# A width-3 convolution by minimal filtering: F(6,3) over 342 tiles in place of F(4,3) over 512

## The chip, the cores and the metric

The kernel runs on one core of a Trainium2 chip. The metric is the device time of one execution in microseconds (us); it was timed in three runs. One further execution was taken by the hardware profiler, and everything below that speaks of a start, a duration or a wait comes from that execution. The engines are named as the profile names them: PE (TensorE, matrix products), PEld (its weight loads), DVE (VectorE), ACT (ScalarE), POOL (GpSimd) and SP (SyncE, which here only issues DMAs).

## The reference

`x` is two sequences of 2048 positions with 1024 channels, bf16; `w` has three taps of 1024x1024. A convolution along the sequence is followed by a batch normalisation and SiLU:

```
xp = pad(x, one position before and after)
y  = sum over k = 0, 1, 2 of  xp[:, k:k+2048, :] @ w[k]
y  = (y - mean) * (g / sqrt(var + 1e-5)) + b
return silu(y)
```

## The kernel before

**The method.** Four neighbouring outputs of a width-3 filter need 12 products of a position with a tap. F(4,3) gets them from 6: each tile of 6 neighbouring positions is combined into 6 sums with the numbers of `BT`, the three taps are combined into 6 weight sums, the 6 pairs are multiplied, and the 4 outputs are sums of the 6 products. Each "product" here is a matrix product over 1024 input channels, done as 8 matrix instructions (one per 128 channels, variable `ct`). A sequence of 2048 has 512 tiles, the two together 1024 (`NT`).

**The first stage** (lines 178 to 233) makes the sums of x. 34 windows of 126 positions are loaded, one DMA each. `Rm` holds the numbers of `BT` laid out for 31 tiles, and a product of the window with `Rm` (line 205, 8 per window) both transposes the window and makes its 6 sums. DVE and ACT share out the copies of the results from PSUM (the banks PE writes) to `T_sb` in SBUF as bf16, two copies of 744 columns per window (lines 217 and 219).

**The weights.** Output channels are worked in 8 chunks of 128 (`dc`). For each chunk the three taps are loaded (`load_weights`, line 133) and POOL makes four weight sums from them (`transform_weights`, line 146): six additions or subtractions of 1024 columns and two multiplications by 2 and 4. The first and last weight sum are the plain taps. The sums live in a pool of two buffers, so those of chunk d+1 can be made while PE works on chunk d.

**The second stage** (lines 288 to 350) goes through units: one unit is one chunk and one block of 512 tiles, so there are two units to a chunk. The very last block is cut into two of 256 tiles. In a unit PE forms the six products `M[1], M[2], M[3], M[4], M[0], M[5]`, 8 instructions of 512 columns each (line 316), in six PSUM banks. ACT copies `M[1]` and `M[3]` to SBUF, DVE combines them with the other products in ten instructions (lines 320 to 337), writing two of the sums back over `M[2]` and `M[4]` in PSUM, and ACT applies scale, bias and SiLU into `yT` (line 306, four instructions). Every one of the ten DVE instructions has one input in PSUM and one in SBUF, or both in PSUM.

**The way out.** `yT` has channels on partitions, the output has positions there. A transposing DMA turns each unit into `o_sb` (line 251), and four DMAs store it (line 247), row by row of the four outputs of a tile. The last two units are transposed by PE instead (line 265) and copied out by DVE and ACT. SP issues these DMAs and the later weight loads in an order that the code fixes with `sp_chain`. A scheduler places the rest: it may move an instruction ahead of others in an engine's queue, and each engine then works its queue strictly in order.

Of the kernel before, what the change touches and what calls it, by code (L numbers as in the profile page):

```python
# [9 lines left out]
ALU = mybir.AluOpType  # L10
# [3 lines left out]

BT = [
    [4, 0, -5, 0, 1, 0],
    [0, -4, -4, 1, 1, 0],
    [0, 4, -4, -1, 1, 0],
    [0, -2, -1, 2, 1, 0],
    [0, 2, -1, -2, 1, 0],  # L20
    [0, 4, 0, -5, 0, 1],
]
KAPPA = [1.0 / 24.0, 1.0 / 12.0, 1.0 / 6.0, 1.0 / 6.0]
WT = 31
# [3 lines left out]
def kernel(  # L28
# [16 lines left out]
    assert S % 4 == 0 and C % P == 0 and D % P == 0  # L45
    NTB = S // 4
    NT = B * NTB
    NWIN = (NTB + WT - 1) // WT
    NBLK = min(512, NT)
    assert NT % NBLK == 0 and NBLK % P == 0  # L50
    NNB = NT // NBLK

# [12 lines left out]
    val = consts.tile([P, 6, WT], I32, name="val")  # L65
    nc.gpsimd.iota(val, pattern=[[-1, 6], [-4, WT]], base=0, channel_multiplier=1)
    E = consts.tile([P, 6, WT], FP32, name="E")
    nc.vector.tensor_single_scalar(E, val, 0.0, op=ALU.is_equal)
    Rm = consts.tile([P, 6, WT], BF16, name="Rm")
    nc.vector.memset(Rm, 0.0)  # L70
    for k in range(6):
        j = 0
        while j < 6:
            v = BT[j][k]
            if v == 0:
                j += 1
                continue
            j1 = j
            while j1 + 1 < 6 and BT[j1 + 1][k] == v:
                j1 += 1  # L80
            nj = j1 - j + 1
            nc.vector.scalar_tensor_tensor(
                out=Rm[:, j:j1 + 1, :],
                in0=E[:, k:k + 1, :].to_broadcast([P, nj, WT]) if nj > 1 else E[:, k:k + 1, :],
                scalar=float(v),
                in1=Rm[:, j:j1 + 1, :],
                op0=ALU.mult,
                op1=ALU.add,
            )
            j = j1 + 1  # L90

# [3 lines left out]
    def load_params(dep=None):  # L95
        prm = consts.tile([P, 4, DC], BF16, name="prm")
        for q, ap in enumerate((var, g, mean, b)):
            d = nc.sync.dma_start(out=prm[:, q, :], in_=ap.rearrange("(dc p) -> p dc", p=P), allow_slow_non_contiguous=True)
            after(d, dep, "param loads happen after the x window loads")
# [3 lines left out]
        nc.gpsimd.tensor_scalar(rstd, prm[:, 0, :], 1e-5, 1.0, op0=ALU.add, op1=ALU.mult)  # L103
        nc.gpsimd.tensor_tensor(rstd, rstd, mhalf, op=ALU.pow)
        sc = consts.tile([P, DC], FP32, name="sc")
        nc.gpsimd.tensor_tensor(sc, prm[:, 1, :], rstd, op=ALU.mult)
        beta = consts.tile([P, DC], FP32, name="beta")
        nc.gpsimd.tensor_tensor(beta, prm[:, 2, :], sc, op=ALU.mult)
        nc.gpsimd.tensor_tensor(beta, prm[:, 3, :], beta, op=ALU.subtract)
        sk = consts.tile([P, DC, 4], FP32, name="sk")  # L110
        for i in range(4):
            nc.gpsimd.tensor_scalar(sk[:, :, i], sc, KAPPA[i], 0.0, op0=ALU.mult, op1=ALU.add)
        return sk, beta

    w_all = w.rearrange("k (ct p) d -> p k ct d", p=P)
    raw = {}
    SYNC_DEP = mybir.DependencyInfo(mybir.DependencyClass.Sync, mybir.DependencyReason.DATA)

    def after(inst, dep, why):
        if dep is not None:  # L120
            tc.add_manual_dep(inst.ins, dep.ins.name, SYNC_DEP, reason=why)


    NOSYNC_DEP = mybir.DependencyInfo(mybir.DependencyClass.NoSync, mybir.DependencyReason.DATA)
    sp_last = [None]

    def sp_chain(inst):
        if sp_last[0] is not None:
            tc.add_manual_dep(inst.ins, sp_last[0].ins.name, NOSYNC_DEP, reason="keep SP DMA issue order")
        sp_last[0] = inst  # L130
        return inst

    def load_weights(dc, dep=None, eng=None, chain=False):
        wch = wpool.tile([P, 3, CT, P], BF16, name="wch")
        if eng is None:
            d = nc.gpsimd.dma_start(out=wch, in_=w_all[:, :, :, dc * P:(dc + 1) * P])  # L136
            after(d, dep, "weight chunk load must not compete with the x window loads")
        else:
            for k in range(3):
                d = eng.dma_start(out=wch[:, k], in_=w_all[:, k, :, dc * P:(dc + 1) * P])  # L140
                after(d, dep, "weight chunk load must not compete with the x window loads")
                if chain:
                    sp_chain(d)
        raw[dc] = wch

    def transform_weights(dc):
        wch = raw[dc]
        uch = upool.tile([P, 4, CT, P], BF16, name="uch")
        g32 = wtmp.tile([P, CT, P], FP32, name="g32")
        f32 = wtmp.tile([P, CT, P], FP32, name="f32")  # L150
        w1x2 = wtmp.tile([P, CT, P], BF16, name="w1x2")
        w2x4 = wtmp.tile([P, CT, P], BF16, name="w2x4")
        w0, w1, w2 = wch[:, 0], wch[:, 1], wch[:, 2]
        nc.gpsimd.tensor_tensor(g32, w0, w2, op=ALU.add)  # L154
        nc.gpsimd.tensor_tensor(uch[:, 0], g32, w1, op=ALU.add)
        nc.gpsimd.tensor_tensor(uch[:, 1], g32, w1, op=ALU.subtract)
        nc.gpsimd.tensor_scalar(w2x4, w2, 4.0, 0.0, op0=ALU.mult, op1=ALU.add)
        nc.gpsimd.tensor_scalar(w1x2, w1, 2.0, 0.0, op0=ALU.mult, op1=ALU.add)  # L158
        nc.gpsimd.tensor_tensor(f32, w0, w2x4, op=ALU.add)
        nc.gpsimd.tensor_tensor(uch[:, 2], f32, w1x2, op=ALU.add)  # L160
        nc.gpsimd.tensor_tensor(uch[:, 3], f32, w1x2, op=ALU.subtract)
        wts[dc] = (wch, uch)

    wts = {}

    T_sb = tpool.tile([P, CT, 6, NT], BF16, name="T_sb")
    CH = 4
    NGRP = 4
    grp_i = 0
    eng_load = {"act": 0.0, "dve": 0.0}  # L170
    EVAC_COST = {"act": 0.80, "dve": 0.95}
    sk = beta = None
    win_i = 0
    xw0 = consts.tile([P, C], BF16, name="xw0")
    nc.gpsimd.memset(xw0[0:1, :], 0.0)
    evacs = []
    NW_TOTAL = B * NWIN
    W0_AFTER = min(8, NW_TOTAL - 1)
    with tc.tile_pool(name="xwin", bufs=12) as xpool:
        for bi in range(B):  # L180
            for wi in range(NWIN):
                ntile = min(WT, NTB - WT * wi)
                n0 = bi * NTB + WT * wi
                t_lo = 4 * WT * wi - 1
                t_hi = 4 * WT * wi + 4 * ntile
                lo = max(t_lo, 0)
                hi = min(t_hi, S - 1)
                p_lo = lo - t_lo
                kk = hi - t_lo + 1
                hi_ld = min(t_lo + P - 1, S - 1)  # L190
                if p_lo > 0:
                    hi_ld = min(hi_ld, lo + 125)
                if p_lo > 0:
                    assert p_lo == 1
                    xw = xw0
                else:
                    xw = xpool.tile([P, C], BF16, name="xw")
                nc.sync.dma_start(out=xw[p_lo:p_lo + (hi_ld - lo + 1), :], in_=x[bi, lo:hi_ld + 1, :])
                win_i += 1
                for h in range(CT // CH):  # L200
                    gi = grp_i % NGRP
                    grp = ps_all[:, gi * 1024:(gi + 1) * 1024].rearrange("p (s e) -> p s e", e=256)
# [181 lines left out]
```

## Time and profile before

| | us |
|---|---|
| three runs, median (lowest to highest) | 211.66 (210.42 to 212.34) |
| span of the profiled execution, first to last instruction | 207.6 |
| median of the runs less that span | 4.06 |
| first product of the second stage starts | 34.86 |
| PE busy | 194.5 (94% of the span) |
| DVE busy | 130.2 (63%) |
| POOL busy | 124.4 (60%) |
| ACT busy | 95.7 (46%) |

The page gives the profiled execution's span and no separate time for it, so what lies around the span is read from the difference to the median of the runs. Rows of a timeline give the start and the duration in us, then engine, line, operation, the tile written and the tiles read, and the count of equal instructions merged into the row. An instruction's duration contains a fixed part that overlaps the next instruction, so two instructions of 0.69 can start 0.60 apart. What a stream of instructions costs is the distance of the starts.

### The profile page before, as it was taken

How to read it: one execution, taken by the hardware profiler on the slowest of the kernel's cores; microseconds unless marked ns; L12 is line 12 of the kernel's file. 1: busy time of each engine (PE TensorE's matmuls, PEld its weight loads, DVE VectorE, ACT ScalarE, POOL GpSimd, SP SyncE). 2: the span in 40 equal slices, each digit the busy share in tenths (PEclk: the TensorE clock that was granted, in tenths of full speed). 3: DMA queues.
4: the chain of work that ended last, by engine and by line, in shares of the span. 5: the costliest groups of instructions: out<-in, count | busy, mean ns of one | idle time of the engine just before them, and what ended most of it. 6: DMA issues, size and time to landing. Idle time of an engine off the chain costs nothing.

```text
span 207.6 us, 3056 instructions
## 1 busy us (share of the span) xinstructions
PE 194.5 (94%) x1104; PEld 104.4 (50%) x1104; DVE 130.2 (63%) x225; ACT 95.7 (46%) x142; POOL 124.4 (60%) x83
## 2 busy tenths in 40 slices
PE   2998788999999999999999999999999999999980
PEld 2977676444444444444444444444444444446870
DVE  5899697292929292929292929292929292929671
ACT  4799697234343434343434333333434343434651
POOL 4030299999999999969925992499469910000000
PEclk9999999999999999999999999999999999999998
DMA  6999972995456945794569457945794545454562
GB/s 190 380 334 312 327 282 2 157 148 104 101 103 156 197 104 101 167 188 101 104 154 200 101 101 167 190 103 101 176 178 104 101 101 101 101 104 101 103 147 56
DMA packets 96035, 31.40 MB, mean 151 GB/s; under 512 B 91606, under 2 KB 91606, under 8 KB 96020
## 3 DMA queue, kind: packets, MB, share of 16 engines
q1 hardware_dynamic: 95812, 30.42, 65.6%
q0 software_dynamic: 208, 0.79, 1.4%
q8 instruction: 8, 0.13, 0.3%
q14 instruction: 7, 0.06, 0.1%
HBM read 14.95 MB, written 8.39 MB: 112 GB/s over the span
## 4 chain that ended last, share of the span: by engine, by line
PE 85%; DMA 6%; ACT 5%; DVE 1%; issue 0%; ACTq 0%; DVEq 0%
PE ps_all L316 79%; ACT T_sb L217 5%; PE ps_all L205 5%; DMA xw<-in_x_dram 5%; DMA xw_105<-in_x_dram 1%; PE ps_all L265 0%; ACT yT L306 0%; ACTq L379 0%; DVE y_1946 L337 0%; DVE cp L325 0%; DVE ps_all L326 0%; DVE y_1946 L331 0%; DVE y_1944 L329 0%; DVE y_1945 L327 0%; DVE o_sb L273 0%
## 5 line engine op out<-in xcount | busy, mean ns | idle before, releaser
L316 PE MATMUL ps_all<-T_sb,uch 128*128 128x512 bf16 (+1 forms) x544 | 113.7, 366 | 0.1
L316 PEld LDWEIGHTS <-uch 128*128 128x128 bf16 x544 | 53.1, 98 | 57.6 <-issue 0.3
L316 PE MATMUL ps_all<-T_sb,wch 128*128 128x512 bf16 (+1 forms) x272 | 58.1, 366 | 0.0
L316 PEld LDWEIGHTS <-wch 128*128 128x128 bf16 x272 | 26.6, 98 | 28.7
L219 DVE CAST T_sb<-ps_all 128x744 bf16<-128x744 f32 (+1 forms) x31 | 26.7, 906 | 4.9 <-PE ps_all L205 4.4
L217 ACT CAST T_sb<-ps_all 128x744 bf16<-128x744 f32 (+1 forms) x37 | 26.7, 786 | 6.3 <-PE ps_all L205 5.8
L205 PE MATMUL ps_all<-Rm,xw 126*128 126x186 bf16 (+1 forms) x256 | 25.4, 250 | 3.8 <-ACT T_sb L217 1.9
L205 PEld LDWEIGHTS <-xw 126*128 126x128 bf16 (+1 forms) x256 | 22.2, 101 | 7.0 <-issue 4.1
L154 POOL TENSOR_TENSOR g_208<-wch 128x1024 f32<-128x1024 bf16 x1 | 2.1, 2115 | 10.0 <-DMA wch<-in_w_dram 10.0
L136 POOL DMA_DIRECT2D wch<-in_w_dram x1 | 1.6, 1639 | 10.3 <-ACT T_sb L217 10.3
L205 PE MATMUL ps_all<-Rm,xw_105 126*128 126x186 bf16 x16 | 2.5, 299 | 3.8 <-DMA xw_105<-in_x_dram 3.7
L158 POOL TENSOR_SCALAR w1x_1291<-wch 128x1024 bf16<-128x1024 bf16 x1 | 1.0, 1045 | 6.0 <-DMA wch<-in_w_dram 6.0
L158 POOL TENSOR_SCALAR w1x_1466<-wch 128x1024 bf16<-128x1024 bf16 x1 | 1.0, 1044 | 5.7 <-DMA wch<-in_w_dram 5.7
L158 POOL TENSOR_SCALAR w1x_1637<-wch 128x1024 bf16<-128x1024 bf16 x1 | 1.0, 1045 | 4.5 <-DMA wch<-in_w_dram 4.5
L205 PEld LDWEIGHTS <-xw_105 126*128 126x128 bf16 x16 | 1.7, 118 | 3.9 <-POOL mhalf L101 3.7
L265 PE MATMUL ps_all<-ident,yT 128*128 128x128 bf16 x16 | 1.6, 220 | 1.6 <-ACT yT L306 1.6
L320 DVE TENSOR_TENSOR bp<-S_582,ps_all 128x512 f32<-128x512 f32 x1 | 0.7, 689 | 3.4 <-PE ps_all L316 3.4
L154 POOL TENSOR_TENSOR g_1464<-wch 128x1024 f32<-128x1024 bf16 x1 | 2.1, 2122 | 1.0 <-DMA wch<-in_w_dram 1.0
L154 POOL TENSOR_TENSOR g_1114<-wch 128x1024 f32<-128x1024 bf16 x1 | 2.1, 2125 | 0.3 <-issue 0.3
L306 ACT ACTIVATE yT<-y_588,beta,sk 128x512 bf16<-128x512 f32 x1 | 0.8, 812 | 3.2 <-DVE y_588 L327 3.2
L158 POOL TENSOR_SCALAR w1x_1116<-wch 128x1024 bf16<-128x1024 bf16 x1 | 1.0, 1046 | 2.0 <-DMA wch<-in_w_dram 2.0
L306 ACT ACTIVATE yT<-y_662,beta,sk 128x512 bf16<-128x512 f32 x1 | 0.8, 815 | 3.1 <-DVE y_662 L327 3.1
(351 smaller groups left out, 301.7 us busy)
## 6 DMA issues: line engine op xcount, KB each, us to landing
xw<-in_x_dram SPq DMA_DIRECT2D x30, 256.0 KB, 6.0
out_dram<-o_sb SPq DMA_DIRECT2D x60, 128.0 KB, 2.2
wch<-in_w_dram SPq DMA_DIRECT2D x21, 256.0 KB, 4.3
wch<-in_w_dram POOLq DMA_DIRECT2D x1, 768.0 KB, 11.5
out_dram<-o_sb SPq DMA_DIRECT2D x8, 64.0 KB, 1.7
xw_105<-in_x_dram SPq DMA_DIRECT2D x2, 252.0 KB
xw<-in_x_dram SPq DMA_DIRECT2D x2, 130.0 KB
o_sb<-yT SPq DMA_TRANSPOSE x15, 4.3
```

The costliest lines, as they stand in the source:

```text
L136: d = nc.gpsimd.dma_start(out=wch, in_=w_all[:, :, :, dc * P:(dc + 1) * P])
L154: nc.gpsimd.tensor_tensor(g32, w0, w2, op=ALU.add)
L158: nc.gpsimd.tensor_scalar(w1x2, w1, 2.0, 0.0, op0=ALU.mult, op1=ALU.add)
L205: nc.tensor.matmul(grp[:, c4, 0:6 * ntile], lhsT=xw[0:kk, ct * P:(ct + 1) * P], rhs=Rm[0:kk, :, 0:ntile], start=True, stop=True,)
L217: ev = nc.scalar.copy(dst, src)
L219: ev = nc.vector.tensor_copy(dst, src)
L265: nc.tensor.transpose(bank_v[:, a, ns, :], yT[:, i, ns * P:(ns + 1) * P], ident)
L306: nc.scalar.activation(yT[:, i, :], src, ACT.Silu, bias=beta[:, dc:dc + 1], scale=sk[:, dc, i:i + 1])
L316: nc.tensor.matmul(M[j], lhsT=lhsT, rhs=T_sb[:, ct, j, nsl], start=(ct == 0), stop=(ct == CT - 1))
L320: nc.vector.tensor_tensor(bp, S1, M[2], op=ALU.subtract)
```

## The change

F(6,3) takes tiles of 8 positions and gets 6 outputs from 8 products. A sequence has 342 tiles (2052 positions, four of them past the end), and a unit is now one chunk and one sequence. The parts:

- `BT` is an 8x8 table, windows hold 21 tiles (still 34 windows), `T_sb` is one tile per sequence with 8 sums.
- Six weight sums are made instead of four. POOL's part is eight additions or subtractions of 1024 columns; the three multiplications go to ACT (`nc.scalar.mul`), the sum `e1` of the outer taps to DVE. For the first chunk DVE does the multiplications and POOL `e1`.
- A unit has 64 matrix instructions of 342 columns in eight PSUM banks, which is all of them. ACT copies three products at once (`Acp`, 1026 columns). DVE forms `S_ = Acp + M` and `D_ = Acp - M` for three pairs at once, in SBUF; twelve `scalar_tensor_tensor` instructions (`stt`, line 268) then make the six outputs from slices of `S_` and `D_`, each reading two SBUF tiles; two additions bring in the products of banks 6 and 7.
- Two SiLU instructions of 3x342 columns write `yT` with the six outputs of a tile interleaved, so that `yT` is in the order of the sequence. The transposing DMA then gives blocks of 128 positions. The SiLU of `D_`'s outputs and the way out are put behind the next unit's `Acp` copy (`late`). The last unit is not cut in two; PE transposes it.
- The first chunk's weights are loaded by SP behind the third window (before: by POOL after eight windows), the parameters by row and transposed by PE, the first window in two DMAs; the manual ordering of DMAs is gone.

The core of the diff:

```diff
 def transform_weights(dc, first=False):
-        nc.gpsimd.tensor_tensor(g32, w0, w2, op=ALU.add)
-        nc.gpsimd.tensor_tensor(uch[:, 0], g32, w1, op=ALU.add)
-        nc.gpsimd.tensor_tensor(uch[:, 1], g32, w1, op=ALU.subtract)
-        nc.gpsimd.tensor_scalar(w2x4, w2, 4.0, 0.0, op0=ALU.mult, op1=ALU.add)
-        nc.gpsimd.tensor_scalar(w1x2, w1, 2.0, 0.0, op0=ALU.mult, op1=ALU.add)
-        nc.gpsimd.tensor_tensor(f32, w0, w2x4, op=ALU.add)
-        nc.gpsimd.tensor_tensor(uch[:, 2], f32, w1x2, op=ALU.add)
-        nc.gpsimd.tensor_tensor(uch[:, 3], f32, w1x2, op=ALU.subtract)
+        for dst, src, f in ((w2x4, w2, 4.0), (w0x4, w0, 4.0), (w1x2, w1, 2.0)):
+            if first:
+                nc.vector.tensor_scalar(dst, src, f, 0.0, op0=ALU.mult, op1=ALU.add)
+            else:
+                nc.scalar.mul(dst, src, f)
+        (nc.gpsimd if first else nc.vector).tensor_tensor(e1, w0, w2, op=ALU.add)
+        nc.gpsimd.tensor_tensor(e2, w0, w2x4, op=ALU.add)
+        nc.gpsimd.tensor_tensor(eh, w0x4, w2, op=ALU.add)
+        for s, op in ((0, ALU.add), (3, ALU.subtract)):
+            nc.gpsimd.tensor_tensor(uch[:, s + 0], e1, w1, op=op)
+            nc.gpsimd.tensor_tensor(uch[:, s + 1], e2, w1x2, op=op)
+            nc.gpsimd.tensor_tensor(uch[:, s + 2], eh, w1x2, op=op)
...
+    def stt(o, i0, s, i1):
+        nc.vector.scalar_tensor_tensor(out=o, in0=i0, scalar=s, in1=i1, op0=ALU.mult, op1=ALU.add)
+
+    units = [(dc, bi) for dc in range(DC) for bi in range(B)]
+    late = []
+    for ui, (dc, bi) in enumerate(units):
...
+        for k, j in enumerate(JA):
+            mms(k, j, dc, bi)
+        nc.scalar.copy(Acp, banks(0, 3))
+        for f in late:
+            f()
+        late = []
+        for k, j in enumerate(JB):
+            mms(3 + k, j, dc, bi)
+        nc.vector.tensor_tensor(S_, Acp, banks(3, 3), op=ALU.add)
+        nc.vector.tensor_tensor(D_, Acp, banks(3, 3), op=ALU.subtract)
+        mms(6, 0, dc, bi)
+        mms(7, 7, dc, bi)
+        for par, src, y in ((0, S_, yS), (1, D_, yD)):
+            for q in range(3):
+                i = 2 * q + par
+                stt(y[:, q], src[:, 1], ALPHA * 2.0 ** i, src[:, 0])
+                stt(y[:, q], src[:, 2], BETA * 0.5 ** i, y[:, q])
+            if par == 0:
+                nc.vector.tensor_tensor(y[:, 0], bank[6], y[:, 0], op=ALU.add)
+                silu(0, yS)
+            else:
+                nc.vector.tensor_tensor(y[:, 2], bank[7], y[:, 2], op=ALU.add)
```

How it moves the queues, at three places. First DVE, from the last copies of the first stage to the end of the first unit, before:

```order
L219 CAST T_sb<-ps_all 128x24x31 x14
L219 CAST T_sb<-ps_all 128x24x16
L320 TENSOR_TENSOR bp<-S_582,ps_all 128x512
L321 TENSOR_TENSOR ps_all<-S_582,ps_all 128x512
L325 TENSOR_TENSOR cp<-S_583,ps_all 128x512
L326 TENSOR_TENSOR ps_all<-S_583,ps_all 128x512
L327 TENSOR_TENSOR y_588<-cp,ps_all 128x512
```

and the same place after the change, where `e_706` and `e_919` are the sums `e1` of the second and the third chunk of weights (one buffer for all of them):

```order
L228 CAST T_sb_138<-ps_all 128x32x6
L141 TENSOR_TENSOR e_706<-wch 128x1024
L141 TENSOR_TENSOR e_919<-wch 128x1024
L296 TENSOR_TENSOR S__617<-Acp,ps_all 128x1026
L297 TENSOR_TENSOR D__618<-Acp,ps_all 128x1026
L268 SCALAR_TENSOR_TENSOR yS<-S__617 128x342 x2
L268 SCALAR_TENSOR_TENSOR yS<-S__617,yS 128x342 x2
L268 SCALAR_TENSOR_TENSOR yS<-S__617 128x342
L306 TENSOR_TENSOR yS<-ps_all,yS 128x342
L268 SCALAR_TENSOR_TENSOR yS<-S__617,yS 128x342
```

The weight sums of two later chunks have come to stand ahead of the first unit's work, and the one input in PSUM that every DVE instruction had is gone from the twelve `L268`. Second, POOL over one chunk of weights in the second stage, before:

```order
L154 TENSOR_TENSOR g_764<-wch 128x1024
L157 TENSOR_SCALAR w2x_767<-wch 128x1024
L158 TENSOR_SCALAR w1x_766<-wch 128x1024
L159 TENSOR_TENSOR f_765<-wch,w2x_767 128x1024
L155 TENSOR_TENSOR uch<-g_764,wch 128x1024
L156 TENSOR_TENSOR uch<-g_764,wch 128x1024
L160 TENSOR_TENSOR uch<-f_765,w1x_766 128x1024
L161 TENSOR_TENSOR uch<-f_765,w1x_766 128x1024
```

and after, for the second and the beginning of the third chunk:

```order
L142 TENSOR_TENSOR e_707<-wch,w2x_711 128x1024
L143 TENSOR_TENSOR eh<-w0x_710,wch 128x1024
L145 TENSOR_TENSOR uch<-e_706,wch 128x1024
L146 TENSOR_TENSOR uch<-e_707,w1x_709 128x1024
L147 TENSOR_TENSOR uch<-eh,w1x_709 128x1024
L145 TENSOR_TENSOR uch<-e_706,wch 128x1024
L146 TENSOR_TENSOR uch<-e_707,w1x_709 128x1024
L147 TENSOR_TENSOR uch<-eh,w1x_709 128x1024
L142 TENSOR_TENSOR e_920<-wch,w2x_924 128x1024
```

The two short multiplications have left POOL and two additions have come; `e_706` is read last by the sixth of the eight, so `e_919`, which takes its buffer, waits for that one. Third, DVE at the start, where the table `Rm` is built, after the change:

```order
L92 SCALAR_TENSOR_TENSOR Rm<-E,Rm 128x21 x6
L138 TENSOR_SCALAR w2x_258<-wch 128x1024
L92 SCALAR_TENSOR_TENSOR Rm<-E,Rm 128x126
L138 TENSOR_SCALAR w0x_257<-wch 128x1024
L138 TENSOR_SCALAR w1x_256<-wch 128x1024
```

A multiplication that waits for the first weights now stands ahead of the last instruction that fills `Rm`, without which PE cannot begin the first stage.

More of the change, by code (lines that the diff above doesn't have):

```diff
@@ L78 @@
             j1 = j
-            while j1 + 1 < 6 and BT[j1 + 1][k] == v:
+            while j1 + 1 < 7 and BT[j1 + 1][k] == v:
                 j1 += 1
@@ L109, in load_params @@
[L109 to L121, printed above, removed]
@@ L124 @@
[L124 to L144, printed above, removed]
@@ L351, with banks, store @@
-    for st, _ in pending:
-        emit_output_stage_pe(st, 0, last=True)
-        emit_output_stage_pe(st, 1, last=True)
+    out_f = out.flatten_outer_dims()
+    bank = [ps_all[:, i * 512:i * 512 + NTB] for i in range(8)]
+    def banks(i0, n):
+        return ps_all[:, i0 * 512:(i0 + n) * 512].rearrange("p (k e) -> p k e", e=512)[:, :, 0:NTB]
+    def store(st, k0, nk):
+        o_sb, dc, bi = st
+        r0 = bi * S + k0 * P
+        dst = out_f[r0:r0 + nk * P, dc * P:(dc + 1) * P].rearrange("(k p) d -> p k d", p=P)
+        nc.sync.dma_start(out=dst, in_=o_sb[:, k0:k0 + nk])
```

344 lines of the change are left out of this document (155 added, 189 removed), and 8 rows, old and new, of the table BT.

## The prediction

> **What bounds the kernel now.** I read the page's busy rows and its chain of work first, then the chain in order of time, then the timeline of one unit, and last the few instructions that resemble those the change brings.
>
> ```profile
> PE 194.5 (94%) x1104; PEld 104.4 (50%) x1104; DVE 130.2 (63%) x225; ACT 95.7 (46%) x142; POOL 124.4 (60%) x83
> PE 85%; DMA 6%; ACT 5%; DVE 1%; issue 0%; ACTq 0%; DVEq 0%
> ```
>
> ```profile
> 0.73 2.88 DMA xw_105<-in_x_dram
> 3.61 0.14 issue
> 3.75 4.51 PE ps_all L205 x28
> ...
> 14.63 10.10 DMA xw<-in_x_dram
> ...
> 34.86 161.67 PE ps_all L316 x776
> 196.54 0.22 PE ps_all L265 x4
> 196.76 1.75 PE ps_all L316 x16
> ```
>
> From 34.86 on the chain is one unbroken run of products: PE bounds the second stage, and nothing stands between its products. The first 34.9 us are loading x and copying its sums. How much a column costs PE is read from two equal points of neighbouring units, the ACT copies of `M[1]`:
>
> ```profile
> 47.78 0.56 ACT L318 COPY S_656<-ps_all 128x512 f32<-128x512 f32 x1
> ...
> 58.14 0.56 ACT L318 COPY S_735<-ps_all 128x512 f32<-128x512 f32 x1
> ```
>
> 10.36 us for 48 instructions of 512 columns is 215.8 ns each; the 16 of 256 columns above took 1.75, 109.4 ns each. Between them lie 0.416 ns a column, so 342 columns should take 109.4 + 86 x 0.416 = 145.1 ns.
>
> **PE's part.** 1024 instructions (8 chunks, 2 sequences, 64) by 145.1 ns are **148.6 us**, 9.29 a unit and 18.6 a chunk. Before, from 34.86 to the end of the last product, it was 166.5:
>
> ```profile
> 199.44 1.91 PE L316 MATMUL ps_all<-T_sb,wch 128*128 128x256 bf16 x16
> ```
>
> This ends at 201.35. If PE stays the bound the products save 17.9 us. Whether it stays the bound is decided by DVE and POOL.
>
> **DVE and POOL per chunk.** One stretch with both at work:
>
> ```profile
> 49.16 0.69 DVE L320 TENSOR_TENSOR bp<-S_656,ps_all 128x512 f32<-128x512 f32 x1 [2.25 <-PE ps_all L316]
> 49.72 2.13 POOL L156 TENSOR_TENSOR uch<-g_561,wch 128x1024 bf16<-128x1024 f32 x1
> 49.76 0.69 DVE L321 TENSOR_TENSOR ps_all<-S_656,ps_all 128x512 f32<-128x512 f32 x1
> 51.81 2.12 POOL L159 TENSOR_TENSOR f_562<-wch,w2x_564 128x1024 f32<-128x1024 bf16 x1
> ...
> 187.68 0.69 DVE L326 TENSOR_TENSOR ps_all<-S_1782,ps_all 128x512 f32<-128x512 f32 x1
> ```
>
> ```profile
> 200.05 0.42 DVE L326 TENSOR_TENSOR ps_all<-S_1940,ps_all 128x256 f32<-128x256 f32 x1
> 200.38 0.41 DVE L327 TENSOR_TENSOR y_1945<-cp,ps_all 128x256 f32<-128x256 f32 x1
> ```
>
> DVE starts are 0.60 apart for 512 columns and 0.33 for 256, so 0.42 for 342, and 1.14 for 1024 or 1026. A unit has two of 1026 and fourteen of 342: 2 x 1.14 + 14 x 0.42 = 8.2; a chunk has two units and one `e1`, 17.5. POOL starts are 2.09 apart; eight are 16.7 a chunk. Against PE's 18.6 each of the two fits, with 1.1 and 1.9 to spare: taken one by one, PE stays the bound. ACT, with two `Acp`, four SiLU and three multiplications of about 1.2 each (0.82 for 512 columns, below), has some 11 a chunk and doesn't matter.
>
> But the two do not work on separate data paths for certain. Before, every DVE instruction of the second stage has an input in PSUM; the 0.69 beside POOL's 2.13 is the 0.69 of 187.68, where POOL has long been done, so such pairs don't disturb DVE. The twelve `L268` a unit and `e1` read two SBUF tiles while POOL reads two as well. The trace has one kind of DVE instruction with two SBUF inputs, the sixteen that build `Rm`, and just one POOL instruction that reads SBUF beside them:
>
> ```profile
> 1.92 0.18 DVE L82 SCALAR_TENSOR_TENSOR Rm<-E,Rm 128x31 bf16<-128x31 f32 x1
> ```
>
> ```profile
> 2.27 0.44 POOL masks.py:199 TENSOR_SCALAR_AFFINE_SELECT ident<-ident 128x128 bf16<-128x128 bf16 x1
> 2.35 0.21 DVE L82 SCALAR_TENSOR_TENSOR Rm<-E,Rm 128x62 bf16<-128x62 f32 x1
> ...
> 2.49 0.27 DVE L82 SCALAR_TENSOR_TENSOR Rm<-E,Rm 128x31 bf16<-128x31 f32 x1
> ```
>
> The instruction of 31 columns takes 0.18 next to a POOL memset (which writes only) and 0.27 inside POOL's select (the 0.21 there has twice the columns). One event of 0.09 us, short, but in the only place where it could show. So I bound the pairing from both sides: at the least nothing, at the most full exclusion, in which DVE's two-SBUF instructions and POOL's never run together. Per chunk that is 16.7 for POOL and 24 x 0.42 + 1.14 = 11.2 for DVE, **27.9 in sequence instead of 18.6**. DVE's other instructions (4 x 1.14 + 4 x 0.42 = 6.2) can hide beside POOL. A gain is excluded. I take the upper end, since the one row that bears on it shows a wait, and a wait that lasts as long as POOL is reading lasts nearly all of the 2.13 us here, whereas the select reads 128 columns once.
>
> [...]
>
> It applies to the weight sums of chunks 3 to 8, made while DVE works on the units of chunks 1 to 7; those of the last chunk leave the final chunk's units free, and those of the second are made largely while DVE waits (next part). That leaves six chunks at 27.9: 6 x 9.3 = **+55.8**.
>
> **The queue of DVE at the turn of the stages.** `e_919` stands ahead of the first `S_` and needs the buffer that POOL's sixth instruction of the second chunk reads last. POOL's chain there begins after ACT's first multiplication behind the last copy (about 1.2), so with products from 35: 35 + 1.2 + 6 x 2.09 = 48.7, then `e_919` 1.14 and `S_`, `D_` 2.28, which is 52.1. PE needs the banks that these free when it comes to the second three products of the second unit, at 35 + 9.3 + 3.5 = 47.8. It waits 4.3, and once more 1.2 at bank 7, which DVE frees 5.9 after 52.1, where PE arrives 4.7 after it. Together **+5.5**. Queued behind `e_919` is all of DVE's work. Bounds: nothing, if POOL starts earlier, and 8.
>
> **The first stage.** The x windows bring the same bytes, and the chain waits on them for 10.10. The copies have 672 columns instead of 744:
>
> ```profile
> L217 ACT CAST T_sb<-ps_all 128x744 bf16<-128x744 f32 x35 | 25.8, 803 | 6.2 <-PE ps_all L205 5.8
> L219 DVE CAST T_sb<-ps_all 128x744 bf16<-128x744 f32 x29 | 25.8, 930 | 4.9 <-PE ps_all L205 4.4
> ```
>
> A tenth off each is 2.6 us. Against it, `Rm` is finished only after the first weights have landed:
>
> ```profile
> wch<-in_w_dram SPq DMA_DIRECT2D x21, 256.0 KB, 4.3
> ```
>
> They are issued when the first window has landed (3.6), so PE begins at about 7.9 instead of 3.75, 4.2 later, while the twelve window buffers go on filling. I put the first product at **35.0**; bounds 33 (the load is hidden) and 39 (all 4.2 added).
>
> **The end.** The last unit is no longer halved. DVE starts on it when sixteen products (2.3 us) are still to come and needs 8.2, so 5.9 after PE's end; then:
>
> ```profile
> 191.66 0.82 ACT L306 ACTIVATE yT<-y_1788,beta,sk 128x512 bf16<-128x512 f32 x1
> 192.38 0.80 ACT L306 ACTIVATE yT<-y_1785,beta,sk 128x512 bf16<-128x512 f32 x1
> ...
> 197.72 0.58 ACT L270 COPY o_sb<-ps_all 128x512 bf16<-128x512 bf16 x1
> ...
> 203.31 0.40 PE L265 MATMUL ps_all<-ident,yT 128*128 128x128 bf16 x4 [0.93 <-ACT yT L306]
> 203.74 0.49 DVE L273 COPY o_sb<-ps_all 128x256 bf16<-128x256 bf16 x2 [0.90 <-PE ps_all L265]
> ```
>
> Two SiLU of 513 columns 1.5, eight transposes 0.8, one copy 0.6, and from the last copy (204.2) to the end of the span 3.4: **12.2**, where 6.3 stood (201.35 to 207.6).
>
> **The sum.** 35.0 + 148.6 + 55.8 + 5.5 + 12.2 = 257.1 as a span, against 207.6. The median of the runs lies 4.06 above the span: 261.2, rounded **261**. Parameters, the interleaved `yT` and the DMAs cost nothing here: a transposing DMA and four stores per unit as before, one unit's time (9.3 or more) to hide in.
>
> **The rivals.**
>
> *DVE and POOL do not disturb each other.* For it: one event of 0.09 us is thin, and the instruction of 0.21 ran inside the same select unharmed. Then 35.0 + 148.6 + 5.5 + 12.2 = 201.3, with 4.1 a time of **205**, 3% faster. It decides at 18.6 a chunk: if a chunk stays below 19.7, the change wins.
>
> *They share, but finer than by whole instructions.* For it: the wait was shorter than the select. Half of the 55.8 gives **233**, slower.
>
> *No disturbance, but DVE becomes the bound by itself.* An instruction that needs the result of the one before it can't use the overlap: 0.42 against a distance of 0.33, 0.09 lost. With ten such in a unit, 8.2 + 0.57 + 0.9 = 9.7 exceeds PE's 9.29 by 0.4, over 16 units 6: **211**, no change. Against it: the scheduler has put other instructions between most of these pairs.
>
> **How the numbers follow.** A measurement of this kernel can tell about 1% from no change. Full exclusion 0.52, sharing 0.14, no disturbance 0.28, DVE alone 0.06: slower 0.66, same 0.06, faster 0.28. The likeliest case's own range is 246 (an exclusion with a quarter of it lost between) to 274 (two us more a chunk, where POOL waits for PE's release of a buffer while DVE has nothing to do). The range has to take in the faster case too: 203 to 274.
>
> **What would show it.** Right: `L268` has a median well above 0.42, some of its instructions over 2 us; POOL's eight are stretched or DVE waits beside them; PE's idle time in the second stage is tens of us, ended by DVE (`S_`, or a bank it frees); six chunks take about 28 and the last one less than 20. `L268` at 0.42 to 0.51 throughout and a chunk of 19 would prove the prediction wrong. The turn of the stages shows as a DVE idle stretch of about 12 us before `e_919`, whose releaser is POOL; the first product of the first stage at about 8 instead of 3.75; and about 12 us between the last product and the end. A product that costs 160 ns rather than 145 would add 15 to every case.

## The result and the profile after

| | before | after |
|---|---|---|
| median of the runs (lowest to highest), us | 211.04 (209.82 to 212.34) | 291.38 (290.77 to 291.77) |
| ratio, 95% interval | | 1.382 (1.375 to 1.390) |
| span of the profiled execution, us | 207.6 | 290.0 |

The medians are of four runs each. The change is 38% slower: the predicted direction, 17 us above the end of the predicted range. Of all runs below, one of a changed kernel (274.83, with six changed `L268`) and one of the kernel before (213.53) lie over 1.5% above the fastest of the same kernel and are left out of times and ratios. The page's busy row:

```profile
PE 203.0 (70%) x1313; PEld 131.1 (45%) x1313; DVE 246.5 (85%) x328; ACT 181.4 (63%) x111; POOL 153.2 (53%) x88
```

PE was busy for 94% of the span and is now for 70%; DVE has gone from 130.2 us to 246.5. Which engine PE waits for, in the view of waits (waiter, releaser, total us, times, longest):

```profile
PE ps_all L265 <- DVE yD L309: 39.2, 13, 13.5
PE ps_all L265 <- DVE yS L306: 14.9, 6, 5.3
PE ps_all L333 <- ACT yT L284: 11.8, 2, 11.1
PE ps_all L214 <- DMA wch<-in_w_dram: 8.2, 1, 8.2
PE ps_all L265 <- DVE D__618 L297: 6.3, 1, 6.3
```

60 us of the second stage are waits for DVE, for the banks 6 and 7 that `L306` and `L309` read and for the one that `D_` reads. The timeline shows what holds DVE up:

```profile
103.31 3.41 DVE L268 SCALAR_TENSOR_TENSOR yS<-S__938 128x342 f32<-128x342 f32 x2
103.94 2.40 POOL L147 TENSOR_TENSOR uch<-eh,w1x 128x1024 bf16<-128x1024 f32 x1
...
106.31 2.39 POOL L145 TENSOR_TENSOR uch<-e,wch 128x1024 bf16<-128x1024 f32 x1
106.64 4.78 DVE L268 SCALAR_TENSOR_TENSOR yS<-S__938,yS 128x342 f32<-128x342 f32 x2
...
108.67 2.38 POOL L146 TENSOR_TENSOR uch<-e,w1x 128x1024 bf16<-128x1024 f32 x1
...
111.35 2.43 DVE L268 SCALAR_TENSOR_TENSOR yS<-S__938 128x342 f32<-128x342 f32 x1
...
114.25 2.44 PE L265 MATMUL ps_all<-T_sb,wch 128*128 128x342 bf16 x8 [5.29 <-DVE yS L306]
```

The two take turns, one instruction each. A `L268` lasts 2.4 us while POOL reads, and POOL's starts are 2.36 apart where they were 2.09 (106.31, 108.67), so that a turn with one instruction of each is only 0.27 longer than POOL's instruction alone. At 114.25 PE has waited 5.29. All 192 `L268` together, in a table of one stretch over the whole span (start and end, its length, DVE's busy time on that line with the count, granted clock, DMA share, GB/s):

```profile
0.00:290.00 290.00, 156.23 (x192) 0.85 0.47 108
```

Where nothing holds them up the same 192 take 85.64 (below), so 70.6 us are waits inside DVE instructions. Six chunks of weights are summed by POOL beside DVE's units, from 56.5 to 241.0, 30.8 us for each chunk; the prediction had 27.9. The last of the six and the chunk after it, in a table of stretches (start and end, length, then the busy time of PE, PEld, DVE, ACT and POOL with their counts, granted clock, DMA share, GB/s):

```profile
210.80:241.00 30.20, 23.19 (x129) 14.02 (x129) 29.12 (x34) 19.69 (x11) 18.14 (x8) 0.84 0.35 70
241.00:261.30 20.30, 20.08 (x130) 12.99 (x129) 16.97 (x32) 16.91 (x8) 0.00 (x0) 0.94 0.40 79
```

Beside POOL's sums DVE is busy for 29.12 of 30.20 us: it has become the bound. The prediction had not looked for the second thing that stands out, in the costliest groups:

```profile
L284 ACT ACTIVATE yT<-yS,beta,sk 128x1026 bf16<-128x1026 f32 x16 | 61.3, 3831 | 67.2 <-DVE yS L268 45.2
L290 ACT COPY Acp<-ps_all 128x1026 f32<-128x1026 f32 x16 | 19.2, 1202 | 0.7 <-PE ps_all L265 0.7
```

A SiLU of 1026 columns takes 3.83 us, three times the copy of the same size and not the 1.2 of the prediction. The products and the turn of the stages:

```profile
36.63 7.13 PE L265 MATMUL ps_all<-T_sb,uch 128*128 128x342 bf16 x48 [0.49 <-ACT T_sb L226]
...
43.60 2.48 PE L265 MATMUL ps_all<-T_sb,wch 128*128 128x342 bf16 x16
...
50.41 3.12 DVE L141 TENSOR_TENSOR e<-wch 128x1024 f32<-128x1024 bf16 x1 [12.43 <-POOL uch L145]
...
55.86 2.44 PE L265 MATMUL ps_all<-T_sb,uch 128*128 128x342 bf16 x8 [6.29 <-DVE D__618 L297]
```

From 36.63 to 43.60 are 48 products, 145.2 ns each. DVE stands for 12.43 before `e_919`, and PE for 6.29 behind it. The end:

```profile
271.21 1.32 PE L265 MATMUL ps_all<-T_sb,wch 128*128 128x342 bf16 x8 [0.37 <-DVE yD L309]
...
281.52 3.79 ACT L284 ACTIVATE yT<-yD,beta,sk 128x513 bf16<-128x513 f32 x2
...
283.66 1.03 PE L333 MATMUL ps_all<-ident,yT 128*128 128x128 bf16 x8 [11.13 <-ACT yT L284]
```

The last product ends at 272.53, 17.5 before the end of the span. Term by term, the collisions being what is left of the second stage:

| term of the sum | predicted | measured |
|---|---|---|
| first product of the second stage | 35.0 | 36.6 |
| 1024 products | 148.6 | 148.7 |
| turn of the stages | 5.5 | 6.3 |
| POOL against DVE | 55.8 | 80.9 (272.53 - 36.63 - 148.7 - 6.3) |
| end | 12.2 | 17.5 |
| median less span | 4.1 | 1.4 |
| sum | 261.2 | 291.4 |

In the 80.9 PE stands still for 54.1 (the 39.2 and 14.9 above). For the rest it is busy: 175.3 in the whole second stage, 26.6 more than 1024 products at 145.2 ns take (last section). The six chunks make up 72.9 of the 80.9 (their 184.5 less six times 18.6); the other 8.0 lie before and behind them.

### The profile page after: what moved, and what is told of

It is laid out like the page before. It is cut to its first block, busy times and chain, and to the rows that moved or that the text cites. A ratio compares the mean times of both kernels' runs of the same rounds, so it can differ in the third digit from the quotient of the medians.

```text
span 290.0 us, 3554 instructions
## 1 busy us (share of the span) xinstructions
PE 203.0 (70%) x1313; PEld 131.1 (45%) x1313; DVE 246.5 (85%) x328; ACT 181.4 (63%) x111; POOL 153.2 (53%) x88
## 5 line engine op out<-in xcount | busy, mean ns | idle before, releaser
L265 PE MATMUL ps_all<-T_sb,uch 128*128 128x342 bf16 x768 | 126.6, 328 | 7.0 <-DVE D__618 L297 6.3
L265 PEld LDWEIGHTS <-uch 128*128 128x128 bf16 x768 | 79.8, 104 | 53.4 <-issue 7.4
L284 ACT ACTIVATE yT<-yS,beta,sk 128x1026 bf16<-128x1026 f32 x16 | 61.3, 3831 | 67.2 <-DVE yS L268 45.2
L265 PE MATMUL ps_all<-T_sb,wch 128*128 128x342 bf16 x256 | 53.1, 363 | 54.1 <-DVE yD L309 39.2
L284 ACT ACTIVATE yT<-yD,beta,sk 128x1026 bf16<-128x1026 f32 (+1 forms) x17 | 61.5, 3638 | 13.3 <-DVE yD L309 13.3
L145 POOL TENSOR_TENSOR uch<-e,wch 128x1024 bf16<-128x1024 f32 x16 | 36.2, 2265 | 23.5 <-PE ps_all L265 16.8
L147 POOL TENSOR_TENSOR uch<-eh,w1x 128x1024 bf16<-128x1024 f32 x16 | 37.7, 2355 | 0.1
L146 POOL TENSOR_TENSOR uch<-e,w1x 128x1024 bf16<-128x1024 f32 x16 | 36.5, 2279 | 0.0
L214 PE MATMUL ps_all<-Rm,xw 128*128 128x168 bf16 (+1 forms) x272 | 25.6, 241 | 10.5 <-DMA wch<-in_w_dram 8.2
L226 ACT CAST T_sb<-ps_all 128x672 bf16<-128x672 f32 (+1 forms) x37 | 24.1, 714 | 10.4 <-PE ps_all L214 9.3
L228 DVE CAST T_sb<-ps_all 128x672 bf16<-128x672 f32 (+1 forms) x31 | 24.2, 838 | 0.9 <-PE ps_all L214 0.7
L141 DVE TENSOR_TENSOR e<-wch 128x1024 f32<-128x1024 bf16 x7 | 10.4, 1489 | 15.6 <-POOL uch L145 12.4
L309 DVE TENSOR_TENSOR yD<-ps_all,yD 128x342 f32<-128x342 f32 x16 | 8.2, 513 | 1.4
L306 DVE TENSOR_TENSOR yS<-ps_all,yS 128x342 f32<-128x342 f32 x16 | 8.0, 503 | 0.0
(129 smaller groups left out, 229.5 us busy)
```

Of the source, the lines that this page charges most:

```text
L145: nc.gpsimd.tensor_tensor(uch[:, s + 0], e1, w1, op=op)
L146: nc.gpsimd.tensor_tensor(uch[:, s + 1], e2, w1x2, op=op)
L147: nc.gpsimd.tensor_tensor(uch[:, s + 2], eh, w1x2, op=op)
L214: nc.tensor.matmul(grp[:, c4, 0:NJ * ntile], lhsT=xw[0:kk, ct * P:(ct + 1) * P], rhs=Rm[0:kk, :, 0:ntile], start=True, stop=True,)
L226: nc.scalar.copy(dst, src)
L228: nc.vector.tensor_copy(dst, src)
```

## The experiments

**SiLU without steps.** `yT` is written as six rows of 342 columns that lie one behind the other; the columns then go out at other positions.

```diff
-        yT_v = yT.rearrange("p (n i) -> p i n", i=M_OUT)
+        yT_v = yT.rearrange("p (i n) -> p i n", i=M_OUT)
```

> Only the order in which SiLU writes yT is changed: the six outputs of the tiles as six contiguous rows instead of interleaved (the output's positions come out permuted). Theory A (DVE's two-input SBUF instructions and POOL's reads exclude each other, and that sets the second stage): the 1026-column SiLU falls from 3.84 us to about 1.25, the contended chunks stay near 28 us, units of the last chunk go from 10.15 to 9.4, time about 262. Rival B (the 3.84 us SiLU, standing ahead of the next Acp copy, is what holds the second stage): time at or below 230.

Measured: 277.55 us, 1.325 (1.317 to 1.334). The group of SiLU:

```profile
L284 ACT ACTIVATE yT<-yS,beta,sk 128x1026 bf16<-128x1026 f32 x16 | 19.9, 1242 | 118.3 <-DVE yS L268 101.3
```

The same work with 1.24 us instead of 3.83, so the step of six elements was the cause. But the kernel gains only 14: it stays 16 above theory A's 262, and far from the rival's 230. The rest is elsewhere. `L268` over the whole span, as above:

```profile
0.00:275.50 275.50, 154.03 (x192) 0.86 0.50 114
```

This is still 68.4 more than 85.64. Together with `e1` (10.4 against 8.5 in the kernel without sums below) 70.3 us of DVE are waits. The second stage, from 36.95 to the last product's end at 262.1, is 225.2 long: 70.2 more than products and turn. The two are nearly equal, but not the same thing. Six chunks beside POOL's sums (56.9 to 229.5) take 28.8 each, together 61.0 more than PE's 18.6; the other 9.2 of the 70.2 lie before and behind them. One of the six, with the columns of the table above:

```profile
112.80:141.60 28.80, 21.78 (x129) 13.42 (x128) 28.56 (x35) 9.56 (x10) 18.24 (x8) 0.86 0.49 101
```

DVE is busy, or held, for 28.56 of 28.80 us. Here too it is the bound, at the price of the collisions.

**POOL without the sums.** The sums of chunks 2 to 8 are left out (every chunk is multiplied with those of the first); once with SiLU as in the change, once with both edits.

```diff
+        if not first:
+            wts[dc] = (wch, uch)
+            return
```

> POOL makes weight sums only for the first chunk; the other chunks multiply with those (the weight sums of chunks 2 to 8 are left out; ACT's multiplications and DVE's e1 stay). Theory A: L268 at 0.50 throughout, every unit at the 10.15 us of the last chunk's, time about 36.6 + 16 x 10.15 + 18 = 218 to 222. Rival B: above 260, since the SiLU stays.

> Both: contiguous SiLU (positions permuted) and no weight sums for chunks 2 to 8. Theory A and B both: PE sets the second stage, units of 9.3 to 9.5, end 13 after the last product: 36.6 + 151 + 13 = 201, time 201 to 206, below the kernel before.

Measured: 224.05 us, 1.067 (1.062 to 1.073), and 200.92, 0.957 (0.953 to 0.961); the first lies 2 above the 222 that was expected at most. Without POOL's reads and without steps F(6,3) comes in below the 205 of the first rival. From the four kernels: the collisions cost 67.3 (291.38 - 224.05) with the steps and 76.6 (277.55 - 200.92) without; the steps cost 13.8 with the collisions and 23.1 without. Each hides some 9 of the other.

**POOL writes and doesn't read.** Each of the eight sums becomes two memsets, so POOL stays busy and its results are no sums.

```diff
+        if not first:
+            for dst in (e2, eh, *(uch[:, s] for s in range(6))):
+                nc.gpsimd.memset(dst, 0.0)
+                nc.gpsimd.memset(dst, 0.0)
+            wts[dc] = (wch, uch)
+            return
```

> POOL's eight additions of each chunk from the second on are replaced by sixteen memsets of the same tiles (the weight sums of chunks 2 to 8 are left out; POOL is about as long at work, writes SBUF and reads none). Theory A in its narrow form (it is the reading that collides): L268 stays at 0.50 beside POOL and the time is that of the run without POOL's sums, 218 to 225. Rival C (any work of POOL beside a DVE instruction with two SBUF inputs collides, or POOL's length sets the chunk): 280 or more, with L268 of 1 us and above.

Measured: 223.83 us, 1.065 (1.061 to 1.070), the time of the kernel without any sums. POOL's memsets, one line of the two, and then the twelve-a-unit instructions over the span (line 274 in this kernel):

```profile
L144 POOL MEMSET uch<- 128x1024 bf16 x42 | 38.8, 953 | 40.1 <-PE ps_all L271 40.1
```

```profile
0.00:221.20 221.20, 85.64 (x192) 0.95 0.62 141
```

112 memsets of 0.95 us beside DVE (84 into `uch`, 28 into `e2` and `eh`), and no `L268` held: 0.446 us each, where one beside POOL's sums took 2.43. In these runs POOL's reads collide with `L268`, its writes don't.

**One SBUF input, for all twelve and for six.** SiLU without steps, POOL in full; `L268` takes one input from a PSUM bank, which makes its result another one. In the second kernel only those of `S_` are changed (the condition `if par else bank[6]`).

```diff
-                stt(y[:, q], src[:, 1], ALPHA * 2.0 ** i, src[:, 0])
-                stt(y[:, q], src[:, 2], BETA * 0.5 ** i, y[:, q])
+                stt(y[:, q], bank[6 + par], ALPHA * 2.0 ** i, src[:, 0])
+                stt(y[:, q], bank[6 + par], BETA * 0.5 ** i, y[:, q])
```

> On top of the contiguous SiLU; POOL does all its weight sums again. Each of the twelve scalar_tensor_tensor of a unit takes its first input from PSUM (the product in bank 6 or 7) instead of from a slice of S_ or D_, so that it has one SBUF input; number, size and order are kept, and the outputs are other numbers. Theory A (the second SBUF input is what collides): the twelve stay at 0.50 us beside POOL's 2.13, time near the run without POOL's sums, 201, plus the stall at the turn of the stages of about 6: 203 to 211. Rival (POOL's reads and DVE collide whatever DVE reads, or POOL's own length sets the chunk): near 277.

> The same for the six instructions that write yS only; the six that write yD keep two SBUF inputs (outputs are other numbers). Theory A with a price by the count of two-input instructions: about half of the way from 277.6 to the other run, 235 to 250. If one two-input instruction per unit is enough to bring POOL and DVE into step: 265 or more.

Measured: 226.23 us, 1.075 (1.072 to 1.079), and 270.38, 1.288 (1.282 to 1.294). Of the first, `L268` over the span:

```profile
0.00:224.10 224.10, 84.99 (x192) 0.95 0.62 140
```

No `L268` is held (0.443 us each), with POOL's reads all there. Of the second:

```profile
0.00:268.50 268.50, 137.09 (x192) 0.88 0.52 117
```

Taking the pairing from half of the instructions removed only 17 of the 68 us of waits. A held `L268` costs 1.93 (2.43 less 0.50), so over six chunks the 51 us left are 4.4 meetings a chunk, and the 68 were 5.9: half as many two-input instructions still meet most of POOL's. In these two kernels the price goes with the number of POOL's instructions that find one. The time fell by only 7, in part because `e1` is held longer (16.2 us in place of 10.4). It lies in the second of the two ranges on record for this kernel, 265 or more; whether one such instruction a unit would do the same was not tried. The first kernel missed: 226 instead of 203 to 211. What is left there:

```profile
L141 DVE TENSOR_TENSOR e<-wch 128x1024 f32<-128x1024 bf16 x7 | 19.6, 2795 | 17.6 <-POOL uch L145 16.4
```

`e1` still reads two SBUF tiles. It takes 2.80 on average instead of 1.22, and DVE stands 16.4 before it for POOL to release its buffer, with the last instructions of a unit behind it. That this is the whole of the 25 us above the kernel with neither price (200.92) was a guess, tested next.

**`e1` on POOL.** As the kernel with twelve changed `L268`, with `e1` moved:

```diff
-        (nc.gpsimd if first else nc.vector).tensor_tensor(e1, w0, w2, op=ALU.add)
+        nc.gpsimd.tensor_tensor(e1, w0, w2, op=ALU.add)
```

> As one_sbuf_all (twelve L268 with one input in PSUM; their results are not the reference's), and e1 made by POOL, so that DVE has no instruction with two SBUF inputs left. Theory A, the 25 us by which one_sbuf_all stood above the kernel without collisions are the six e1, their wait for POOL's buffer and what stands behind them in DVE's queue: 201 to 208, L268 at 0.50 throughout and no unit above 9.6. Rival, those 25 us are POOL's work itself: nine sums instead of eight make it longer still, 228 to 235.

Measured: 204.34 us, 0.972 (0.969 to 0.976), with one more sum a chunk on POOL. The groups show POOL's sums at 2.18 and `L268` at 0.51, so neither holds the other up:

```profile
L145 POOL TENSOR_TENSOR uch<-e,wch 128x1024 bf16<-128x1024 f32 x16 | 34.9, 2180 | 0.0
L268 DVE SCALAR_TENSOR_TENSOR yD<-ps_all,yD 128x342 f32<-128x342 f32 x48 | 24.4, 507 | 0.6
```

The guess holds for the most part: seven instructions on DVE were worth 22 of the 25 us. That POOL's own work sets the time, the rival, is out.

**A second buffer for `e1`**, in the kernel of the change, to take away the wait at the turn alone:

```diff
+    wtmp2 = ctx.enter_context(tc.tile_pool(name="wtmp2", bufs=2))
-        e1 = wtmp.tile([P, CT, P], FP32, name="e1")
+        e1 = wtmp2.tile([P, CT, P], FP32, name="e1")
-        w1x2 = wtmp.tile([P, CT, P], BF16, name="w1x2")
+        w1x2 = wtmp2.tile([P, CT, P], BF16, name="w1x2")
```

> The changed kernel as it is, with two buffers for e1 and for the doubled middle tap, so that DVE's and ACT's work for the third chunk of weights no longer waits for POOL's last reads of the second. The step of the prediction: DVE's idle 12.4 us ahead of it goes, the time falls by about 5.5, to 285. Rival: nothing to be measured, 290 to 292, because DVE then meets POOL's reads twelve us earlier and pays there.

Measured: 289.80 us, 1.378 (1.374 to 1.381), not to be told from the change's 1.382 (1.375 to 1.390). The wait is gone: the costliest groups show no idle time before `e1`, and PE's 6.3 for `D_` is no longer among its waits. The first row is `e1`, the second the twelve a unit over the span (line 269 here):

```profile
L142 DVE TENSOR_TENSOR e<-wch 128x1024 f32<-128x1024 bf16 x7 | 10.3, 1490 | 0.0
```

```profile
0.00:287.80 287.80, 163.27 (x192) 0.85 0.47 109
```

7.0 more than the 156.23 of the change. DVE starts earlier, finds POOL reading, and pays there what it has saved.

**The price of a step.** In the kernel without sums, SiLU writes with a step of one, two, three and six elements in the chunks in turn (positions permuted accordingly):

```diff
-        yT_v = yT.rearrange("p (n i) -> p i n", i=M_OUT)
+        lay = dc % 4
...
+            if lay == 0:
+                o = yT.rearrange("p (r q n) -> p r q n", r=2, q=3)[:, par, :, n0:n1]
...
+            elif lay == 1:
+                o = yT.rearrange("p (q n r) -> p r q n", r=2, q=3)[:, par, :, n0:n1]
...
+            elif lay == 2:
+                o = yT.rearrange("p (r n q) -> p r q n", r=2, q=3)[:, par, :, n0:n1]
...
+            else:
+                o = yT.rearrange("p (n q r) -> p r q n", r=2, q=3)[:, par, :, n0:n1]
```

> The run without POOL's later weight sums, with four layouts of yT in turn by chunk (positions permuted, weight sums of chunks 2 to 8 left out): SiLU writes with a step of 1, 2, 3 and 6 elements of 2 bytes. [...] If it slows with the step: about 1.24, 1.8, 2.3 and 3.84. Time between 201 and 224.

Measured: 209.70 us, 0.998 (0.995 to 1.001). The groups of the four lines, from a step of six (`L300`) down to one of one (`L291`):

```profile
L300 ACT ACTIVATE yT<-yS,beta,sk 128x1026 bf16<-128x1026 f32 x4 | 15.3, 3831 | 7.3 <-DVE yS L271 3.9 <-issue 3.4
...
L297 ACT ACTIVATE yT<-yS,beta,sk 128x1026 bf16<-128x1026 f32 x4 | 8.5, 2129 | 14.0 <-DVE yS L271 14.0
...
L294 ACT ACTIVATE yT<-yS,beta,sk 128x1026 bf16<-128x1026 f32 x4 | 6.3, 1582 | 10.4 <-DVE yS L271 7.8 <-DMA o_sb<-yT 2.5
...
L291 ACT ACTIVATE yT<-yS,beta,sk 128x1026 bf16<-128x1026 f32 x4 | 5.0, 1244 | 16.2 <-DVE yS L271 15.6 <-ACT w1x L140 0.6
```

1.24, 1.58, 2.13 and 3.83 us for steps of one, two, three and six elements: in these rows of ACT's the time grows with the step from two elements on. For two and three elements 1.8 and 2.3 were on record, 0.2 more than measured.

**A kernel without either price.** The whole computation by F(6,3): `S_` of the second and third pair is written over its products in PSUM, `D_` over the banks from which `Acp` was copied, so that each `stt` has one PSUM and one SBUF input; which bank has which part changes from unit to unit, so that PE finds free banks. `e1` is POOL's. ACT copies one product at a time. SiLU writes six rows, padded to 384 columns (18 blocks of 128 to transpose instead of 16), and the stores put the positions in order.

```diff
-        nc.vector.tensor_tensor(S_, Acp, banks(3, 3), op=ALU.add)
-        nc.vector.tensor_tensor(D_, Acp, banks(3, 3), op=ALU.subtract)
...
+        nc.vector.tensor_tensor(D0, Acp[:, 0], bank[b0], op=ALU.subtract)
+        nc.vector.tensor_tensor(S0, Acp[:, 0], bank[b0], op=ALU.add)
+        for k, (aa, bb) in ((1, (a1, b1)), (2, (a2, b2))):
+            mms(bb, JB[k], dc, bi)
+            nc.vector.tensor_tensor(bank[aa], Acp[:, k], bank[bb], op=ALU.subtract)
+            nc.vector.tensor_tensor(bank[bb], Acp[:, k], bank[bb], op=ALU.add)
...
+        a0, a1, a2, b0, b1, b2, z7, z0 = a0, b0, a1, a2, z7, b1, b2, z0
```

> The whole of the reference with F(6,3), arranged so that no DVE instruction of the second stage has two SBUF inputs: S[1], S[2] are written over the products in PSUM, D[1], D[2] over the banks from which Acp was copied, the banks change their parts from unit to unit, POOL makes e1 (nine sums a chunk, 9 x 2.09 = 18.8 us beside PE's 18.6), and SiLU writes rows without steps (columns padded to 384, so 18 blocks of 128 instead of 16). Theory A, all that F(6,3) lost was lost to pairs of two-input instructions and to the steps of SiLU's output: first product 36.6, products 148.6, POOL some 4 to 6 behind in all, end 10, some 1.5 outside the span: 200 to 208. Rival B, DVE is the bound once it reads PSUM twenty times a unit (20 x 0.5 = 10.0 against 9.3): about 215. Rival C, POOL's reads hold up DVE whatever its inputs are: 260 or more.

Measured: 204.75 us, 0.976 (0.972 to 0.981): 2 to 3% below the kernel before, and within theory A's range. One piece of its chain in order of time, and then one chunk with the columns of the tables above:

```profile
60.83 124.56 PE ps_all L272 x856
```

```profile
98.00:116.60 18.60, 18.60 (x130) 12.42 (x129) 17.55 (x42) 9.94 (x13) 18.60 (x10) 1.00 0.81 167
```

PE runs without a gap again, with POOL just as full beside it and DVE at 17.55 of 18.60, which leaves room for two more instructions of 0.42 a chunk.

**The same with the change's layout.** `yT` interleaved, 16 blocks and four stores, nothing else changed:

```diff
-                yT[:, par::2, 0:NTB], src, ACT.Silu, bias=beta[:, dc:dc + 1], scale=sk[:, dc:dc + 1]
+                yT_v[:, par::2, 0:NTB], src, ACT.Silu, bias=beta[:, dc:dc + 1], scale=sk[:, dc:dc + 1]
```

> psum_slices (the whole of the reference, no DVE instruction with two SBUF inputs) with yT interleaved again in the order of the sequence and the 16 blocks and four stores of the change: both SiLU of a unit write with a step of six elements. Theory A, the layout costs by itself: ACT has 2 x 3.84 for SiLU, some 1.2 for the three copies and half of 3.1 for the multiplications in each unit, 10.4 against PE's 9.29, so 16 x 1.1 = 18 more and some 4 more at the end: 222 to 230, slower than the kernel before. Rival B, the prediction's view that the interleaved yT costs nothing because ACT is not on the path: 204 to 210.

Measured: 230.97 us, 1.099 (1.092 to 1.106). Of PE's waits the two longest, and 100 us of the second stage (columns as above):

```profile
PE ps_all L264 <- DVE yD L267: 18.9, 6, 4.6
PE ps_all L338 <- ACT yT L286: 10.3, 1, 10.3
```

```profile
100.00:200.00 100.00, 87.53 (x567) 56.55 (x566) 76.64 (x181) 89.29 (x58) 74.60 (x36) 0.95 0.61 122
```

ACT is the busiest engine, and the layout alone costs 26 us; the time lies 1 above theory A's upper end.

**The late start of PE.** The faster kernel again, with the first chunk's three multiplications on POOL, so that `Rm` is ready early:

```diff
-                nc.vector.tensor_scalar(dst, src, f, 0.0, op0=ALU.mult, op1=ALU.add)
+                nc.gpsimd.tensor_scalar(dst, src, f, 0.0, op0=ALU.mult, op1=ALU.add)
```

> psum_slices with the first chunk's three multiplications on POOL instead of DVE, so that no instruction that waits for the first weights stands ahead of the last one that fills Rm. PE's first product should start at 4 to 4.5 instead of 8.5. Theory A, the late start is added in full to the first stage, whose copies then run without a gap: its last copy and the second stage's first product 4 earlier, 199 to 202. Rival B, the windows of x then set the pace of the first stage (its chain in the kernel before waited 10.10 for them) and take the 4 back: 203.5 to 205. In between, POOL's first chunk of sums is three multiplications longer and may hold up the second stage by 1.

Measured: 204.63 us, 0.975 (0.972 to 0.978), no different. PE's timeline:

```profile
4.75 3.52 PE L214 MATMUL ps_all<-Rm,xw 128*128 128x168 bf16 x24 [4.75 <-DVE Rm L92]
10.93 2.42 PE L214 MATMUL ps_all<-Rm,xw 128*128 128x168 bf16 x16 [2.66 <-DMA xw<-in_x_dram]
...
37.28 7.13 PE L272 MATMUL ps_all<-T_sb,uch 128*128 128x342 bf16 x48 [0.24 <-ACT T_sb L226]
```

and without the edit:

```profile
8.48 3.97 PE L214 MATMUL ps_all<-Rm,xw 128*128 128x168 bf16 x32 [8.48 <-DMA wch<-in_w_dram]
...
36.89 7.13 PE L272 MATMUL ps_all<-T_sb,uch 128*128 128x342 bf16 x48 [0.49 <-ACT T_sb L226]
```

PE starts 3.7 earlier, waits for a window at 10.93, and the second stage begins no earlier. In this kernel the wait for the weights had cost nothing.

## Why the prediction was right in kind and wrong in size

- **PE's part**: 145.1 ns a product worked out from two sizes, 145.2 measured. Right.
- **The exclusion**: right. The long chunks come from `L268` of 2.4 us beside POOL's reads; with one SBUF input (84.99) or with POOL only writing (85.64) no `L268` is held. That the wait lasts for a whole instruction of POOL, on which the 27.9 rests, was the author's estimate from one wait of 0.09 us; no row of the kernel before shows it. The runs nearly do: 2.43 against 0.50, 1.93 more beside POOL's 2.13. The rivals of no disturbance and of finer sharing fall. So does DVE as the bound by itself: without POOL's sums and without steps the time is 200.92, not 211.
- **"The interleaved `yT` cost nothing"; ACT "some 11 a chunk and doesn't matter"**: wrong, a term put at nothing, and the largest single part of the miss of 30. SiLU with a step of six elements is 3.83, not 1.2, so ACT has 21 a chunk (four SiLU 15.3, two copies 2.4, three multiplications 3.3), more than PE's 18.6. Taking the steps away, one changed line, was worth 13.8 us. Of the 80.9, 10.7 go with them: the next `Acp` stands behind a SiLU in ACT's queue, and `S_` waits for it (11.7 us in nine units by the view of waits). By itself, in the kernels without collisions, the layout costs 23 to 26. The 1.2 was taken from a SiLU whose output had no step: the row was of the right operation and the wrong access pattern.
- **27.9 a chunk, +55.8**: the exclusion right, the sum not; measured 80.9. The sum took the two engines' exclusive times in sequence and let everything else fit in between. The step that failed is "DVE's other instructions (6.2) can hide beside POOL". In the trace DVE is full: it has its own 17.5 a chunk and is held on top, and each POOL instruction that meets a waiting `L268` costs it 1.93. 70.3 us of waits over six chunks are 11.7 each, about six such meetings of the eight possible. 17.5 + 11.7 = 29.2 is the chunk of the kernel without steps (28.8 above). That 27.9 lies so near to it is partly luck: hiding the 6.2 made the sum too short, all eight meetings made it too long. Of the 25.1 by which this term is too small, the longer chunk (28.8 for 27.9) accounts for some 5 and the steps for some 12 (30.8 for 28.8). The remaining 8 lie outside the six chunks, where the sum has nothing; what they consist of was not taken apart.
- **The end, 12.2**: 17.5; 13.4 in the kernel of SiLU without steps (262.1 to 275.5). 4 of the 5 missing are the steps again.
- **The turn, +5.5**: there (12.4 for DVE and 6.3 for PE, releaser POOL as named), but not an addend. With the wait removed the time moved by 1.6, less than can be told: work that starts earlier runs into POOL earlier. A wait ahead of a contended stretch is worth only what the stretch leaves of it.
- **The first stage, 35.0**: PE began at 8.2 as worked out (7.9), the second stage at 36.6. The late start is hidden, which the last experiment shows. Counted from PE's first product the stage takes 28.4, 2.7 less than before, as the smaller copies should have it, but it ends no earlier; with the early start of the last experiment it takes 32.5. What sets its end is open.
- **Median less span**, 4.06: a wrong reading. It sets the median of three runs against the span of another, faster execution. In every run that has both, of either kernel, time and span are 1.7 to 1.9 apart; the profiled execution of the change took 291.77 for its 290.0.
- **The range**, 203 to 274, had its upper end from two more us a chunk (its own terms give 273, and 247 for the 246). The bounds of that term covered how the two engines share, but not that a second, unlooked-at term (ACT) could be wrong at the same time.

That F(6,3) itself is no loss is shown by the kernel without either price: 2.4% below F(4,3), at the 205 of the first rival. Its second stage is 152.0 long (36.89 to 188.86), 3 more than the products. Most of that, two waits of 0.66 and 2.06, lies at the turn of the stages, where its chain goes through POOL's sums.

## What to carry to other kernels

Before moving DVE inputs from PSUM to SBUF, look at what POOL reads at that time: beside a stream of POOL's reads each meeting costs DVE nearly a whole POOL instruction (1.93 of 2.13 here), and six two-input instructions a unit were enough for most of the price (51 of 68 us of waits). Price an operation by a row with the same access pattern, not only the same operation and size (a SiLU of 1026 columns took 1.24 or 3.83 us here). When an engine's slack is as thin as DVE's 1.1 of 18.6, add up its work with the waits on top, rather than fitting it into the gaps of another.

## What the runs showed that was not expected

- ACT's time for 1026 columns by the step of its bf16 output: 1.24, 1.58, 2.13, 3.83 us for 1, 2, 3 and 6 elements.
- POOL pays little in the exchange: 2.39 and a distance of 2.36, where it has 2.13 and 2.09 alone. DVE pays 2.43 for 0.50.
- PE's products are often slower after waits. At 114.25, after 5.29 of waiting, 8 products are listed with 2.44; at 271.21, after 0.37, 8 take 1.32. It is not the length of the last wait alone: at 145.47, after 2.52, 8 again take 1.32. The granted clock of the change is 0.849 over the span, that of the kernel without either price 0.975. In the six chunks DVE sets the time, so most of the 26.6 us that PE is slower should be hidden there; how much it costs by itself was not tried.
